# Block-diagonal attention matmuls, split input loads and DMA transposes in a fused linear-attention and MLP kernel

## The chip, the cores and the metric

The kernel runs on one core of a Trainium2 chip. The metric is the device time of the whole program in microseconds (us), the slowest core's, which here is the only core. The times quoted are medians of several executions. TensorE is called PE here, its weight loads PEld, VectorE DVE, ScalarE ACT, GpSimd POOL and SyncE SP. Every run also lists the mean granted TensorE clock, where 1.0 is full speed. A run that is over 1.5% above the fastest of its kernel counts as slow and is left out of the ratios; the others are the fast runs.

## The reference, cut to what matters

```python
# q, k, v: (8, 8, 576, 64) = (batch B, head H, token S, D), float32
q_s = softmax(q, axis=-1)                              # over D
k_s = softmax(k, axis=2)                               # over tokens
kv  = np.einsum('bhsd,bhse->bhde', k_s, v)             # 64 x 64 a head
o   = np.einsum('bhsd,bhde->bhse', q_s, kv)
x   = o.transpose(0, 2, 1, 3).reshape(4608, 512)       # heads side by side
h   = x @ w_in                                         # 512 x 2048
g   = np.where(h > 0, h, np.exp(np.minimum(h, 0)) - 1) # ELU
out = g @ w_out                                        # 2048 x 512
```

Nearly all arithmetic is in the two MLP products: 9 blocks of 512 tokens, 64 matmuls of 128x512 for the hidden layer and 64 for the output in each, 1152 in all.

## The kernel before

A *unit* is four heads of one batch, so there are 16 units, n = 0 to 15. The MLP runs in groups of eight matmuls: `hg(j, g)` is a hidden group of block j, `out_mm` an output group. The attention of later batches is put between those groups as *pieces*: transposes of q (`tp`), the product k^T v (`kv`), and two output pieces (`ao`). A small list scheduler inside the program fixes the order of instructions on each engine ahead of time, from assumed durations and an assumed DMA rate.

The load of q, k or v of a unit is one transfer of 590 KB (576 KB in the profile's units) that fills all 128 partitions. Partition half f (64 partitions) holds the heads f and 2+f of the four, one in each slot h:

```python
def load(self, n, t, key, eng="gp"):
    b, u = n // 2, n % 2
    i = n % 2
    src = self.src[t][b, 4 * u:4 * u + 4, :, :].rearrange(
        "(h f) (p c) d -> (f p) h (c d)", f=2, c=CH)      # head = 2h + f
    dst = self.RAW[i][t][:, :, :, :].rearrange("p h c d -> p h (c d)")
    # [cut] self.S.add(eng, ..., e.dma_start(dst, src), ...)
```

The order of two heads, f and 2+f, in one column block means that their outputs belong to different 128-row chunks of x. So the output piece uses four matmuls in row tiles of 64 partitions, which put heads 2h and 2h+1 together:

```python
def ao(self, n, x, ps, key, evac="act"):
    # [cut]
    for f in range(2):
        for h in range(2):
            hs = slice(h * 64, h * 64 + 64)
            e.matmul(P[:, h * 512:h * 512 + n_], M[hs, f, :],
                     T[hs, c0:c1, f * 64:f * 64 + 64], start=(f == 0), stop=(f == 1))
```

`kv` is called once a unit, 36 small matmuls each. `tp` makes nine PE transposes and one ACT eviction a unit. Loads, and the weights W1 and W2 behind them, stand in one POOL queue in the order of use; only q of unit 0 goes through SP.

The softmax here doesn't subtract the row's maximum and nothing guards it: scores larger than these inputs give would overflow.

## Time and profile before

| | before |
|---|---|
| time, median of 3 | 329.84 us (329.71 to 330.46) |
| span of the profiled execution | 328.2 us, clock 1.0 |
| first MLP matmul | 18.62 us |
| PE busy | 95% |
| PE waits after the first MLP matmul | 5.7 us (sum of the waits view from 18.7 us on) |

The waits of PE, longest in total first (total us, times, longest). The first two belong to the head of the program, with 0.2 us more of it not shown; the waits after the first MLP matmul sum to 5.7:

```profile
PE PS L354 <- ACT QR L320: 5.5, 1, 5.5
PE PS L385 <- ACT VB L331: 1.9, 1, 1.9
PE PS L444 <- DVE GT L459: 1.4, 2, 1.1
PE PS L475 <- DVE GT L465: 1.3, 1, 1.3
```

A unit of attention in steady state, from the timeline of PE (start, length, line, operation, tile, count): two output pieces, transposes and kv stand between MLP groups, and the groups beside the pieces last 2.09 to 2.12 us, where undisturbed ones (from 203.02 us on) last 1.98 and start 1.81 us apart.

```profile
183.34 0.50 PE L417 MATMUL PS<-qsT,MBLK 64*128 64x256 f32 x4
183.78 2.12 PE L444 MATMUL PS<-XT,W 128*128 128x512 f32 x8
185.74 0.68 PE L367 MATMUL PS<-ID,QS 128*128 128x128 f16 x9
186.22 2.09 PE L475 MATMUL PS<-W,GT 128*128 128x512 f32 x8
188.25 0.48 PE L385 MATMUL PS<-VB,KR 64*64 64x65 bf16 x36
188.66 2.12 PE L444 MATMUL PS<-XT,W 128*128 128x512 f32 x8
```

### The profile page before, as it was taken

Reading aid. Unit: us, or ns where it says so; the run is one execution under the profiler, and the core shown is the slowest. Engines: PE = TensorE matmul, PEld = TensorE weight load, DVE = VectorE, ACT = ScalarE, POOL = GpSimd, SP = SyncE. Lnnn points to the kernel's source line nnn. Section 1 sums busy time; section 2 is a strip of 40 time slices with the busy share of each in tenths; the row PEclk is TensorE's granted clock in tenths of the full one; section 3 lists DMA queues with packets and bytes.
Section 4 is the critical chain, followed back from the end, with each engine's and each line's share of the span. In section 5 each row is a group of like instructions: output and inputs, shape, how many; then the busy total and the mean of one; then the engine's idle time right before and its main releaser. Section 6 shows DMA issues by size and latency. Waiting matters only on the chain.

```text
span 328.2 us, 4867 instructions
## 1 busy us (share of the span) xinstructions
PE 310.5 (95%) x2090; PEld 241.3 (74%) x2090; DVE 191.2 (58%) x236; ACT 166.5 (51%) x190; POOL 70.7 (22%) x86
## 2 busy tenths in 40 slices
PE   3799999978999999999999999999999999999895
PEld 3677767655777776787778777877888888888683
DVE  4548844698877587667666546455455545554400
ACT  3835646996667467546744563444333343334211
POOL 8732443895403421304020020000000000000000
PEclk9999999999999999999999999999999999999999
DMA  7999999656636827623542130210121111112122
GB/s 235 396 386 389 390 358 323 191 178 211 206 121 217 247 42 241 213 70 104 176 149 61 34 105 7 56 35 13 39 49 32 32 34 32 32 34 59 37 64 64
DMA packets 17045, 46.45 MB, mean 142 GB/s; under 512 B 2048, under 2 KB 2048, under 8 KB 17024
## 3 DMA queue, kind: packets, MB, share of 16 engines
q0 software_dynamic: 10992, 36.11, 34.5%
q1 hardware_dynamic: 6032, 10.03, 12.2%
q8 instruction: 16, 0.26, 0.3%
q14 instruction: 5, 0.04, 0.0%
HBM read 36.70 MB, written 9.44 MB: 141 GB/s over the span
## 4 chain that ended last, share of the span: by engine, by line
PE 83%; DVE 7%; DMA 4%; ACT 3%; issue 1%; POOL 1%; SPq 0%; POOLq 0%
PE PS L475 39%; PE PS L444 36%; PE PS L417 4%; DMA VR<-in_v_dram 2%; DVE GT L459 2%; PE PS L367 2%; PE PS L385 2%; DMA out_dram<-OSB 1%; DVE QS L341 1%; ACT ESB L452 1%; DVE ZQ L333 1%; DVE GT L465 1%; POOL ESB L457 1%; ACT OSB L488 1%; PE PS L354 0%
## 5 line engine op out<-in xcount | busy, mean ns | idle before, releaser
L444 PE MATMUL PS<-XT,W 128*128 128x512 f32 x576 | 144.5, 395 | 2.8 <-DVE GT L459 1.4
L475 PE MATMUL PS<-W,GT 128*128 128x512 f32 x576 | 145.4, 396 | 1.3 <-DVE GT L465 1.3
L444 PEld LDWEIGHTS PS<-XT,W 128*128 128x128 f32 x576 | 106.0, 188 | 27.0 <-DVE GT L459 2.0
L475 PEld LDWEIGHTS PS<-W,GT 128*128 128x128 f32 x576 | 105.8, 188 | 25.6 <-issue 1.8
L452 ACT ACTIVATE ESB<-PS 128x1024 f32<-128x1024 f32 x72 | 73.8, 1026 | 89.8 <-PE PS L444 88.6
L463 DVE TENSOR_SCALAR ESB<-ESB 128x1024 f32<-128x1024 f32 x61 | 45.1, 740 | 70.1 <-ACT ESB L452 70.1
L465 DVE TENSOR_TENSOR GT<-ESB,PS 128x1024 fp32r<-128x1024 f32 x61 | 74.5, 1221 | 2.1
L488 ACT ACTIVATE OSB<-PS 128x512 f32<-128x512 f32 x36 | 21.5, 597 | 38.1 <-PE PS L475 36.1
L333 DVE TENSOR_REDUCE ZQ<-QR 128x18 f32<-128x1152 f32 x16 | 21.6, 1350 | 19.0 <-ACT QR L320 19.0
L320 ACT ACTIVATE QR<-QR 128x1152 f32<-128x1152 f32 x16 | 18.7, 1166 | 14.1 <-DMA QR<-in_q_dram 13.9
L328 POOL CAST VB<-VR 128x1152 bf16<-128x1152 f32 x15 | 18.4, 1230 | 31.7 <-PE PS L385 29.4
L293 POOL DMA_DIRECT2D QR<-in_q_dram x15 | 11.1, 738 | 64.8 <-DVE QS L341 57.3
L341 DVE TENSOR_TENSOR QS<-QR,RZQ 128x1152 f16<-128x1152 f32 x15 | 21.8, 1453 | 5.4 <-PE PS L367 5.2
L427 ACT ACTIVATE XT<-PS 128x640 fp32r<-128x640 f32 (+3 forms) x31 | 20.1, 650 | 7.1 <-PE PS L417 7.1
L370 ACT ACTIVATE qsT<-PS 128x1152 fp32r<-128x1152 f16 x15 | 17.0, 1130 | 6.3 <-PE PS L367 6.2
L324 ACT ACTIVATE KR<-KR 128x1152 bf16<-128x1152 f32 x16 | 18.6, 1161 | 1.8 <-DMA KR<-in_k_dram 1.7
L459 DVE SCALAR_TENSOR_TENSOR GT<-ESB,PS 128x1024 fp32r<-128x1024 f32 x11 | 13.4, 1217 | 6.0 <-POOL ESB L457 5.9
L417 PEld LDWEIGHTS PS<-qsT,MBLK 64*128 64x128 f32 x120 | 8.9, 185 | 10.2 <-issue 4.6
L417 PE MATMUL PS<-qsT,MBLK 64*128 64x320 f32 (+3 forms) x120 | 16.0, 345 | 0.0
L457 POOL TENSOR_SCALAR ESB<-ESB 128x1024 f32<-128x1024 f32 x11 | 12.3, 1119 | 15.3 <-ACT ESB L452 15.2
L293 POOL DMA_DIRECT2D KR<-in_k_dram x16 | 12.0, 748 | 7.3 <-PE PS L385 7.3
L354 PE MATMUL PS<-ID 128*128 128x128 f16 x90 | 7.3, 249 | 5.5 <-ACT QR L320 5.5
(30 smaller groups left out, 81.6 us busy)
## 6 DMA issues: line engine op xcount, KB each, us to landing
KR<-in_k_dram POOLq DMA_DIRECT2D x16, 576.0 KB, 5.2
VR<-in_v_dram POOLq DMA_DIRECT2D x16, 576.0 KB, 6.9
out_dram<-OSB SPq DMA_DIRECT2D x72, 128.0 KB, 2.4
QR<-in_q_dram POOLq DMA_DIRECT2D x15, 576.0 KB, 5.0
W<-in_moe_w_in_dram POOLq DMA_DIRECT2D x4, 1024.0 KB, 15.6
W<-in_moe_w_out_dram POOLq DMA_DIRECT2D x4, 1024.0 KB, 23.0
QR<-in_q_dram SPq DMA_DIRECT2D x1, 576.0 KB, 3.5
```

Source lines behind the costliest of these rows:

```text
L293: S.add(eng, ISSUE[eng], lambda e: e.dma_start(dst, src), key, W=[f"{t}R{i}"], dma=f"{t}{i}{eng}", nbytes=128 * 4608, follow=self.gpq if c ...
L333: S.add("dve", t_dve(1152), lambda e: e.tensor_reduce(self.ZQ[i][:, :, :].rearrange("p h c -> p (h c)"), raw["q"][:, :, :, :].rearrange("p ...
L341: S.add("dve", t_dve(1152), lambda e: e.tensor_tensor(qso, raw["q"][:, :, :, :], rz, ALU.mult), key - 3, R=rr("q") + [f"RZQ{i}"], W=[f"QS{ ...
L417: last = e.matmul(P[:, h * 512:h * 512 + n_], M[hs, f, :], T[hs, c0:c1, f * 64:f * 64 + 64], start=(f == 0), stop=(f == 1))
L427: S.add("act", t_act(2 * n_, True), lambda e: e.activation(dst, src, AF.Copy), key, W=W, X=banks)
L444: last = e.matmul(P[:, t * 512:(t + 1) * 512], self.W1[:, kc, tt * 128:(tt + 1) * 128], self.XT[:, kc, rc:rc + BLK], start=(kc == 0), stop ...
L452: S.add("act", t_act(1024, True), lambda e: e.activation(esb[:, :], P[:, :], AF.Exp), key, W=[f"E{i}"], X=banks)
L459: S.add("dve", t_dve(1024) + 60, lambda e: e.scalar_tensor_tensor(gt, esb[:, :], -1.0, P[:, :], ALU.add, ALU.max), key, R=[f"E{i}"], W=gw, ...
L463: S.add("dve", t_dve(1024, 2), lambda e: e.tensor_scalar(esb[:, :], esb[:, :], 1.0, -1.0, ALU.min, ALU.add), key, X=[f"E{i}"])
L465: S.add("dve", t_dve(1024) + 60, lambda e: e.tensor_tensor(gt, esb[:, :], P[:, :], ALU.max), key, R=[f"E{i}"], W=gw, X=banks)
L475: last = e.matmul(dst, GT[:, jj, ts * 128:(ts + 1) * 128], self.W2[:, jj, :], start=(jj == 0), stop=(jj == 15))
L488: S.add("act", t_act(512, True), lambda e: e.activation(osb[:, :], src, AF.Copy), key, W=[f"O{i}0", f"O{i}1"], X=[f"b{bk}"])
```

## The change

The intent is to take attention work off PE, the busiest engine. Two *adjacent* heads are put in one column block (head = 2f+h), so that one 128x128 block-diagonal matrix M replaces the tiled matmuls, two untiled matmuls for four tiled ones. `kv` runs once a batch (72 matmuls at once) from batch 2 on. The transposes of q from batch 2 on move to the DMA engines (issued from SP), with a POOL cast after them. The pieces stand at fixed steps of the MLP, and the scheduler's durations are new. The core of the diff:

```diff
-    def load(self, n, t, key, eng="gp"):
-        src = self.src[t][b, 4 * u:4 * u + 4, :, :].rearrange(
-            "(h f) (p c) d -> (f p) h (c d)", f=2, c=CH)
-        dst = self.RAW[i][t][:, :, :, :].rearrange("p h c d -> p h (c d)")
+    def load_half(self, n, t, f, eng, key, after=(), follow=None):
+        h0 = 4 * u + 2 * f
+        src = self.src[t][b, h0:h0 + 2, :, :].rearrange("h (p c) d -> p h (c d)", c=CH)
+        dst = self.RAW[i][t][f * 64:f * 64 + 64, :, :, :].rearrange("p h c d -> p h (c d)")
 ...
     def ao(self, n, x, ps, key, evac="act"):
-            for f in range(2):
-                for h in range(2):
-                    hs = slice(h * 64, h * 64 + 64)
-                    last = e.matmul(P[:, h * 512:h * 512 + n_], M[hs, f, :],
-                                    T[hs, c0:c1, f * 64:f * 64 + 64], start=(f == 0), stop=(f == 1))
+        for f in range(2):
+            def mm(e, f=f):
+                return e.matmul(P[:, f * 512:f * 512 + n_], M[:, f, :],
+                                T[:, c0:c1, f * 64:f * 64 + 64], start=True, stop=True)
 ...
+        if dmat:                                   # batches 2 to 7
+            t16 = self.raw_flat(i, "q").bitcast(F16)[:, 0:1152].rearrange("p (c t) -> p c t", c=CH)
+            S.add("sp", ISSUE["sp"], lambda e: e.dma_start_transpose(
+                t16, self.QS[al][:, :, :].rearrange("p c x -> p (c x)")), key, ...)
 ...
+        for m, (n, t) in enumerate(order):         # the head: units 0 and 1
+            sp = first[n, t] = self.load_half(n, t, 0, "sp", -70 + m, follow=sp)
+            ac = self.load_half(n, t, 1, "act", -70 + m, follow=ac)
+        self.load_w1(0, -60, after=[first[0, "v"]])
 ...
+            self.load_half(n, t, 1, "gp", ...)     # units 2 to 15
+            self.load_half(n, t, 0, "sp", ...)
```

With head = 2f+h the 128 partitions of a load no longer step evenly through memory, so the one transfer becomes two, each to 64 partitions. The bytes are the same.

## The prediction

> **What bounds it now.** TensorE. The page's first part has PE busy 95% of 328.2 us, DVE 58%, ACT 51%, at full clock. The timeline shows a head of 18.62 us before the first MLP matmul, 305.5 us of middle, and a tail of 4.0 us. Undisturbed groups of eight MLP matmuls start 1.81 us apart (203 to 216 us), so the 1152 need 261 us: a floor. Of the other 44 us of the middle about 6 are PE waits (waits view) and 37 attention on PE: at 183.3 to 193.2 us one unit (four heads) costs 9.89 - 4 x 1.81 = 2.63 us, 14 times. Transposes are 0.48 of it, kv 0.41, two output pieces 0.92; the other 0.8 is MLP groups stretched from 1.81 to about 2.04 us beside pieces, which I read as 0.09 on entering a tiled piece and 0.14 on leaving. [...]
>
> **What the change does.**
> - Output pieces: 2 untiled matmuls for 4 tiled ones[...]: 0.3 to 0.45 us against 0.46 plus 0.2.
> - kv once a batch: 0.82 + 0.23 us against 2 x (0.41 + 0.23).
> - Transposes of batches 2 to 7 leave PE (0.48 + 0.13 us a unit) and ACT (1.13 us). In their place: an SP-issued DMA transpose and a POOL cast of about 1.2 us. [...] The order leaves about 10.
> - So a batch costs PE 2.3 to 2.9 us, not 5.26: six save 14 to 18. Units 2 and 3 save 1.2.
> - DVE work is spread. The chain runs through DVE from 59 to 73 us and PE loses about 2.6 there; perhaps 2 come back.
> - New wait: after block 1, the second half output group follows the last hidden group by 2.2 us, while exp 1.03, POOL min 1.04 and DVE 1.22 need over 3.3: 1 to 1.5 us, once. Later boundaries leave 3.6 against 3.2: up to 0.5 each.
> - Head: v of unit 1 now reaches its matmul at 15.5 us, after a 1.16 us POOL cast. Loads on SP and ACT and a split cast should start the MLP at about 16: 2.5 saved.
> - Tail: two groups fill the 1.29 us wait before the last output; the last stores issue from two engines: 1.8 saved.
>
> **On the critical path.** Nearly all. Head 16 + MLP 261 + attention 20 + waits and small losses 5.5 + tail 3.5 = 306 us of span, plus 1.6 by which time exceeds span: 307.5 us, 7% less; range 302 to 313. Faster by over 2% 0.96, within 0.03, slower 0.01.
>
> **In the profile, if right.** First MLP matmul at 15.5 to 17 us. Groups beside output pieces at 1.81 us, stretched only around kv. Output matmuls start 0.15 to 0.23 us apart. [...] PE never waits behind the cast. A wait of 1 to 1.5 us after block 1, about 5 in all. The last wait of 1.29 gone.
>
> **What would make it wrong.** Slow DMA transposes; SP blocked behind them, and then stores, output buffers and PE; DVE slowed by POOL's added casts (a QS multiply takes 1.36 to 2.0 us); waits at every block boundary; ACT-issued loads delaying the head.

The 0.09 and 0.14 us are the estimate from the trace before, where groups beside tiled pieces last 2.09 to 2.12 us and undisturbed ones 1.98. "The order leaves about 10" means 10 us for a transpose and its cast. The sum: it adds up to 306 us of span, and with the 1.6 to 307.5 us (rounded).

## More of the kernel before

The page's first two parts. The first line gives busy time, share of the span and number of instructions; the others cut the span in 40 slices of 8.2 us, with busy tenths, granted clock in tenths, DMA engines' busy tenths, and the GB/s that moved:

```profile
PE 310.5 (95%) x2090; PEld 241.3 (74%) x2090; DVE 191.2 (58%) x236; ACT 166.5 (51%) x190; POOL 70.7 (22%) x86
...
PE   3799999978999999999999999999999999999895
...
PEclk9999999999999999999999999999999999999999
DMA  7999999656636827623542130210121111112122
GB/s 235 396 386 389 390 358 323 191 178 211 206 121 217 247 42 241 213 70 104 176 149 61 34 105 7 56 35 13 39 49 32 32 34 32 32 34 59 37 64 64
```

PE is the limit nearly everywhere. But read the last line too: from 8 to 49 us the DMA engines are full, at 358 to 396 GB/s, and PE only just gets its data. After some 60 us there is plenty of room.

The page's list of DMA issues, with KB each and the median us from issue to landing:

```profile
KR<-in_k_dram POOLq DMA_DIRECT2D x16, 576.0 KB, 5.2
VR<-in_v_dram POOLq DMA_DIRECT2D x16, 576.0 KB, 6.9
...
QR<-in_q_dram POOLq DMA_DIRECT2D x15, 576.0 KB, 5.0
...
W<-in_moe_w_out_dram POOLq DMA_DIRECT2D x4, 1024.0 KB, 23.0
```

## The result, and the profile after

The changed kernel is correct and takes 344.54 us (343.46 to 347.64, 4 runs), against 330.15 us (329.71 to 332.08, 4 runs) for the kernel before on the same chip. The ratio of the two is 1.044, with a 95% interval of 1.038 to 1.050: it is slower by 4.4%, where 6.8% faster was predicted. All ratios here are the mean time of one kernel's fast runs over the mean of the other's fast runs of the same rounds, so they are not quite the ratio of the medians. The granted clock was 0.964 or 0.965 in the runs of the changed kernel, and 1.0 in the profiled run before.

The same parts of the page:

```profile
PE 301.1 (88%) x1898; PEld 242.7 (71%) x1898; DVE 194.9 (57%) x240; ACT 152.0 (44%) x178; POOL 76.7 (22%) x93
...
PE   1689467678887988999999999999999999899995
...
PEclk9879959988999999999999999999999999999999
DMA  7999999987698589459656944841212111111133
GB/s 180 303 368 269 247 272 224 250 213 203 137 231 150 106 206 214 123 129 255 151 109 169 238 110 126 204 101 42 57 44 47 34 31 31 31 33 31 31 77 78
```

PE does less work, and in the first third it is idle more often and its granted clock is under 0.9 in five of the 13 slices, at the lowest 0.50 (42.7 to 51.3 us). The DMA engines are as busy as before there (9 tenths), but in four of the five slices from the second to the sixth they move 247 to 303 GB/s, where the kernel before moved 358 to 396. They are busy longer, for the same inputs. The list of issues: half the size, and hardly an earlier landing (q from POOL, not shown, takes 5.2 us):

```profile
QR<-in_q_dram SPq DMA_DIRECT2D x16, 288.0 KB, 4.8
KR<-in_k_dram SPq DMA_DIRECT2D x16, 288.0 KB, 6.5
VR<-in_v_dram SPq DMA_DIRECT2D x16, 288.0 KB, 8.5
W<-in_moe_w_out_dram POOLq DMA_DIRECT2D x4, 1024.0 KB, 29.7
...
KR<-in_k_dram POOLq DMA_DIRECT2D x14, 288.0 KB, 5.6
VR<-in_v_dram POOLq DMA_DIRECT2D x14, 288.0 KB, 6.8
```

The waits of PE. The second and the fifth line belong to the head. From the first MLP matmul on, at 23.22 us, they sum to 26.3 us (with the 0.6 us just before that matmul), against 5.7 before:

```profile
PE PS L516 <- DVE GT L499: 9.0, 2, 7.3
PE PS L467 <- ACT QR L323: 7.1, 1, 7.1
PE PS L483 <- DVE GT L506: 4.0, 5, 1.3
PE PS L483 <- ACT XT L459: 3.7, 1, 3.7
PE PS L399 <- POOL VB L363: 3.2, 1, 3.2
PE PS L516 <- DMA W<-in_moe_w_out_dram: 3.1, 1, 3.1
```

The longest wait, 7.3 us, is put down to DVE, but DVE is not its cause. The timelines of ACT and of PE (in brackets, the idle time before and what ended it) show the chain behind it:

```profile
41.08 1.16 ACT L323 ACTIVATE QR<-QR 128x1152 f32<-128x1152 f32 x1 [7.42 <-DMA QR<-in_q_dram]
42.14 1.92 ACT L491 ACTIVATE ESB<-PS 128x1024 f32<-128x1024 f32 x2
```

```profile
45.58 5.49 PE L516 MATMUL PS<-W,GT 128*128 128x512 f32 x12 [7.33 <-DVE GT L499]
```

In the program's order for ACT, the exponential of q of unit 2 stands ahead of two exponentials of MLP block 0, and ACT waits 7.4 us for its data; so the MLP exponentials, DVE after them, and PE after that, all wait for a load of q. The 12 matmuls after the wait then take 5.49 us, where 12 at full speed take 2.72 (12 times the 1.81/8 of an undisturbed group). The granted clock was 0.50 in that stretch (windows view, 45.5 to 51.1 us), and 0.56 in the 4.5 us before it, in which PE was idle; it had been 1.00 from 37 to 41 us. What lowers it, the runs do not show.

The chain of waits that ends last, in the stretch from 25 to 70 us, is made of loads of v and of W1 (start, length, what):

```profile
18.00 10.98 DMA W<-in_moe_w_in_dram
...
30.29 15.62 DMA VR<-in_v_dram
...
47.47 21.12 DMA VR<-in_v_dram
```

Later, PE does its work as fast as was predicted, or faster. A block of 16 MLP groups and one batch of attention takes 31.15 us (149.67 to 180.82), of which 16 x 1.814 = 29.02 is MLP, so this batch costs PE 2.13 us, against 2 x 2.63 = 5.26 before. The groups beside its output pieces last 1.98 to 2.01 us, like undisturbed ones; the one after kv lasts 2.11:

```profile
149.67 0.78 PE L399 MATMUL PS<-VB,KR 64*64 64x65 bf16 x72
150.38 2.11 PE L516 MATMUL PS<-W,GT 128*128 128x512 f32 x8
...
159.90 1.98 PE L483 MATMUL PS<-XT,W 128*128 128x512 f32 x8
161.72 0.41 PE L440 MATMUL PS<-qsT,MBLK 128*128 128x256 f32 x2
161.96 2.01 PE L516 MATMUL PS<-W,GT 128*128 128x512 f32 x8
```

So the picture is: the gain that was sought is there, 3.13 us a batch, or 18.8 us in all if all six batches are like this one, and then about 33 us were lost elsewhere, most of it before 110 us.

### The profile page after: what moved, and what is told of

Same layout as the page of the kernel before. It is cut to its first block, busy times and chain, and to the rows that moved or that the text cites. A ratio compares the mean times of both kernels' runs of the same rounds, so it can differ in the third digit from the quotient of the medians.

```text
span 341.7 us, 4607 instructions
## 1 busy us (share of the span) xinstructions
PE 301.1 (88%) x1898; PEld 242.7 (71%) x1898; DVE 194.9 (57%) x240; ACT 152.0 (44%) x178; POOL 76.7 (22%) x93
## 4 chain that ended last, share of the span: by engine, by line
PE 62%; DMA 22%; DVE 6%; POOL 3%; ACT 2%; issue 2%; SPq 2%; ACTq 0%; POOLq 0%
PE PS L516 31%; PE PS L483 29%; DMA VR<-in_v_dram 14%; DMA W<-in_moe_w_in_dram 3%; DMA QR<-QS 2%; DVE GT L506 2%; DMA out_dram<-OSB 2%; PE PS L440 2%; ACT ESB L491 2%; DMA QR<-in_q_dram 1%; SPq L284 1%; DVE ESB L503 1%; POOL VB L363 1%; DVE QS L333 1%; POOL qsT L347 1%
## 5 line engine op out<-in xcount | busy, mean ns | idle before, releaser
L516 PEld LDWEIGHTS PS<-W,GT 128*128 128x128 f32 x576 | 108.6, 192 | 35.3 <-DVE GT L499 9.9
L506 DVE TENSOR_TENSOR GT<-ESB,PS 128x1024 fp32r<-128x1024 f32 x63 | 76.9, 1221 | 2.2
L347 POOL CAST qsT<-QR 128x1152 fp32r<-128x1152 f16 x12 | 15.4, 1285 | 88.5 <-PE PS L440 73.1
L357 ACT ACTIVATE KR<-KR 128x1152 bf16<-128x1152 f32 x16 | 18.5, 1164 | 12.5 <-DMA KR<-in_k_dram 12.4
L363 POOL CAST VB<-VR 128x1152 bf16<-128x1152 f32 x15 | 17.5, 1191 | 12.8 <-DMA VR<-in_v_dram 12.8
L459 ACT ACTIVATE XT<-PS 128x640 fp32r<-128x640 f32 (+4 forms) x30 | 18.6, 620 | 1.4 <-PE PS L440 1.4
L440 PE MATMUL PS<-qsT,MBLK 128*128 128x320 f32 (+5 forms) x64 | 14.9, 321 | 4.2 <-ACT XT L459 2.5
L440 PEld LDWEIGHTS PS<-qsT,MBLK 128*128 128x128 f32 x64 | 12.1, 198 | 8.6 <-ACT XT L459 3.6
L284 POOL DMA_DIRECT2D KR<-in_k_dram x14 | 9.3, 666 | 39.2 <-PE PS L399 39.2
L496 POOL TENSOR_SCALAR ESB<-ESB 128x1024 f32<-128x1024 f32 x9 | 9.9, 1097 | 20.9 <-ACT ESB L491 20.9
L499 DVE SCALAR_TENSOR_TENSOR GT<-ESB,PS 128x1024 fp32r<-128x1024 f32 x9 | 11.0, 1220 | 6.1 <-POOL ESB L496 6.0
L412 DVE RECIPROCAL RZK<-PS 128x2 f32<-128x2 f32 x16 | 2.7, 168 | 19.9 <-PE PS L399 19.7
```

The costliest lines, as they stand in the source:

```text
L347: self.S.add("gp", 1250, lambda e: e.tensor_copy(dst, src), key, R=[f"qR{i}0", f"qR{i}1"], W=["qsT0"], low=True, tag=f"cvt{n}")
L363: S.add("gp", 1250, lambda e: e.tensor_copy(VB[:, :, :, 0:D], raw[:, :, :, :]), key, R=rv, W=[f"VB{i}0", f"VB{i}1"], low=True, tag=f"cv{n}")
L440: return e.matmul(P[:, f * 512:f * 512 + n_], M[:, f, :], T[:, c0:c1, f * 64:f * 64 + 64], start=True, stop=True)
L506: S.add("dve", t_dve(1024), lambda e: e.tensor_tensor(gt, esb[:, :], P[:, :], ALU.max), key, R=[f"E{i}"], W=gw, X=self.banks(ps), tag=f"el ...
L516: last = e.matmul(dst, GT[:, jj, ts * 128:(ts + 1) * 128], self.W2[:, jj, :], start=(jj == 0), stop=(jj == 15))
```

## The experiments

The theories:

- **T1**: the loads are slow because each transfer fills 64 of the 128 partitions.
- **T2**: they are slow because of the queues that issue them (SP and ACT in place of POOL).
- **T3**: they are not slow; they only come in a bad order, or the engines' order is wrong. A later form, **Theory B** against it, says that the data come too late at any order.
- **T4**: the DMA transposes disturb the loads.

### e1: the loads by themselves

A measuring kernel, with a wrong output, repeats the loads of units 0 and 1 (3.54 MB) in eight forms, one after the other, with waits between, then the DMA transposes.

```diff
+ full loads:  POOL | SP | SP and ACT
+ half loads:  SP + ACT | SP + POOL | both POOL | both SP | lower half only, SP
+ DMA transposes of q, SP
```

> A measuring kernel, wrong output on purpose: ten phases of loads alone, each begun when the one before has landed. T1 (a load that fills only 64 of 128 partitions is slow): the full loads of phases 1 to 3 run at about 390 GB/s on any queue, the lower halves alone (phase 8) at about 200 to 235, and halves from two queues (4, 5) in between. T2 (the SP and ACT queues are slower than POOL's): phases 2, 3, 4 and 8 at about 235, phases 1 and 6 (both from POOL) at about 390. T3 (rates are equal, only order and gates differ): every phase at about 390 GB/s. Phases 9 and 10: transposes land in 3 to 4 us alone, and slow the loads beside them by no more than their bytes if they are harmless.

The windows view, in the order above (stretch and length; busy time of DVE and POOL, with nothing of note; clock; DMA engines' busy share; GB/s):

```profile
...
18.00:24.00 6.00, 0.00 (x0) 0.00 (x0) 1.00 1.03 380
30.00:36.00 6.00, 0.00 (x0) 0.00 (x0) 1.00 1.05 401
42.00:50.00 8.00, 0.00 (x0) 0.00 (x0) 1.00 1.05 281
...
91.00:101.00 10.00, 0.00 (x0) 0.00 (x0) 1.00 1.04 234
107.00:112.00 5.00, 0.00 (x0) 0.00 (x0) 1.00 1.04 208
116.00:121.00 5.00, 0.00 (x0) 0.00 (x0) 1.00 0.97 220
```

Three forms are left out of the fence: whole loads from POOL, whose first issue still lies in the stretch that was read (350 GB/s), halves on SP and POOL (286), and both halves on POOL (235). The whole transfers move 380 to 401 GB/s from SP or SP and ACT, so the queues are not at fault and T2 falls. Halves move 281 to 286 when two queues carry one half each, 234 to 235 from one queue, and 208 when only one half is loaded. In all of them the DMA engines are busy all the time (1.03 to 1.05). So the engines are not idle; each byte takes longer. T3, that the loads are not slow, falls as a whole explanation too. The last line of the fence is the transposes alone; phase 10, transposes beside loads, is read under e6.

One queue with both halves gave 234 against 208 for one half alone, 13% more, and two queues gave 281, 35% more, though far from 401. Why half of the partitions, or half of the size, is slower, no run here shows.

### e2: whole loads in the changed kernel

Each pair of half loads becomes the wide load of the kernel before. Heads are then paired wrongly and the output is wrong; the work is the same. The edit also takes the later loads off SP, and with them the wait for W1 that the SP halves had, so e2 alone does not part the form of the loads from their order; e1 and e3 are needed beside it.

```diff
-    self.load_half(n, t, 1, "gp", key); self.load_half(n, t, 0, "sp", key)
+    self.load_full(n, t, "gp", key)     # "(h f) (p c) d -> (f p) h (c d)", 128 partitions
```

> The changed kernel with each q, k and v load as one 128-partition load (SP and ACT in turn in the head, POOL later); heads are paired as before, so the output is wrong on purpose. T1: most of the loss comes back, head at 17 to 18 us, PE waits between 35 and 80 us under 6 us, time 308 to 318 us. T2: the head stays at about 22 us and only the later stalls go: about 325. T3 (it is the order of pieces and gates): 338 us or more.

The fast runs were 319.88 and 320.58 us, a ratio of 0.970 [0.966, 0.973] to the kernel before. Two more runs, 326.93 and 327.93, count as slow. So by its fast runs the change with whole loads is 3% faster than the kernel before, and about 24 us faster than with half loads (17 us by the slow ones). That lies between the theories' numbers: T1 expected 308 to 318 us and a head of 17 to 18 us (20.14 measured), T2 about 325 us and a head of 22. The DMA line of the page is again like that of before, up to 390 GB/s, and the clock is full:

```profile
PEclk9999999999999999999999999999999999999999
DMA  7999998954965644783595437313111112011132
GB/s 278 292 351 390 388 390 319 283 137 152 257 154 151 246 120 129 245 194 97 120 289 174 112 82 218 109 33 72 33 33 36 33 44 51 7 33 33 46 86 69
```

PE's waits after the head are 12.5 us in place of 26.3 (in both with the 0.6 us just before the first MLP matmul).

### e3: half loads in the kernel before

The other direction: the kernel before, with only its loads split by partition half. It is correct, since the order of heads is kept.

```diff
-    e.dma_start(dst, src)                       # 128 partitions, POOL
+    for f, eng in ((0, "sp"), (1, "gp")):       # 64 partitions each
+        e.dma_start(RAW[f * 64:f * 64 + 64], src[f])
```

> The kernel before with each load cut into a lower half from SP and an upper half from POOL, all else the same. T1: the head and the first 80 us become slow as in the changed kernel, 338 us or more. T2: half of the bytes slow, about 335. T3: within 1% of before.

It took 359.72 us (357.76 to 360.23), a ratio of 1.087 [1.083, 1.092]: the split, with half of each load moved to SP, costs the kernel before 29 us. PE then waits for W1 (4.4 us) and W2 (4.8 us), which stand behind the slow loads. e1, e2 and e3 together show the split loads as the main cause: they are slow by themselves, taking the split away gives back 24 us, and putting it into the other kernel costs 29. That it is the 64 partitions of T1, and not the smaller size of each transfer, e2 and e3 do not tell apart (see e13).

### e4 and e5: which loads

e4 has whole loads for units 0 and 1 only, e5 for units 2 to 15 only. Both outputs are wrong, as in e2.

```diff
 e4: - load_half(n, t, 0, "sp"); load_half(n, t, 1, "act")     # head only
     + load_full(n, t, "sp" or "act")
 e5: - load_half(n, t, 1, "gp"); load_half(n, t, 0, "sp")      # all but the head
     + load_full(n, t, "gp")
```

> The changed kernel with full loads for units 0 and 1 only (wrong output on purpose for these); the later loads stay halves from SP and POOL. By the half-load theory the head falls from 23.2 to about 20.1 us and the stalls between 38 and 80 us stay: 340 to 342 us, so the head is the small part of the loss.

> The changed kernel with halves for units 0 and 1 only, full loads from POOL later (wrong output on purpose). Head about 23 us as in the changed kernel, the stalls after it mostly gone: 322 to 326 us. If instead head and later losses only shift into each other, this and the run with a full head both stay near 340.

e4: 343.77 us, ratio 1.041 [1.035, 1.047], within a us of the changed kernel. e5: 325.83 us, ratio 0.985 [0.979, 0.991]. e5 is as expected, though "unclear" as a verdict at 2%. In e4 the first MLP matmul came at 21.8 us, not at 20.1, and what was gained was lost in the next wait, a single one of 12.9 us, before which ACT waits 9.3 us for q of unit 2. So the head alone brings nothing. The loads after the head bring 19 us, and the head 5 us more on top of them (e2).

### e6: PE transposes in place of DMA transposes

e2, with the transposes of batches 2 to 7 back on PE and their eviction on ACT (output wrong, as in e2). The pieces move to other steps to make room for them.

```diff
-    self.q_part(n0, first_step, True);  self.cvt(n0, first_step)
+    self.q_part(n0, first_step, False); self.tp(n0, AT, key)
```

> All loads full as in e2, and the transposes of batches 2 to 7 put back on PE with an ACT eviction. If DMA transposes are as good as free there, this is slower than e2's fast runs (320) by the PE time of 12 transposes, 12 x 0.48 to 0.61 = 6 to 7 us: about 326. If the transposes' small packets or the POOL cast cost time in e2, it is slower by less, or faster.

328.01 us (327.14 to 329.05), about 8 us above e2's fast runs. So with whole loads the DMA transposes are worth their place. And in the changed kernel the first of them leaves at 78.93 us, after the late head and after 16.6 of the 26.3 us of PE's waits, so T4 cannot be the cause of that part of the loss.

But transposes beside loads are not harmless. Alone a transpose lands in 2.9 us (e1, phase 9). In phase 10 two transposes and four whole loads, 2.96 MB in all, took 20 us (121.6 to 141.6), where the rates measured alone, 220 and 380 GB/s, give an estimate of 9; one transpose landed after 5.3 us and one after 16.9. "No more than their bytes" was missed, and no run tells why. In the changed kernel transposes land in 2.9 to 8.1 us; how much of its 9.1 us of waits after 79 us is theirs was not tested.

### e7: whole loads only at the start

A first correct try at a better kernel: units 0 to 3 with whole loads and the tiled output pieces of the kernel before, half loads and the block-diagonal form from batch 2 on; head on SP; pieces of unit 3 earlier.

```diff
+NOLD = 4                              # units below: load_full, 4 tiled ao matmuls
-            6: lambda: (self.ao(2, 0, AT, key), loads(4, "kv", key)),
+            5: lambda: (self.ao(2, 0, AT, key), loads(4, "kv", key)),
```

> A correct version: units 0 to 3 with full loads and the tiled output matmuls of before, the head's loads all on the SP queue in order, halves with block-diagonal matmuls from batch 2 on, pieces of unit 3 one step earlier, the first output groups of block 1 reordered to give the last hidden group 3.6 us, block 8 starting with one hidden group. If half loads cost only while DMA is the limit (first 60 us), this is faster than e2: head 17 us, 309 to 315 us. If halves hurt in the steady part too, 318 or more.

327.45 us, ratio 0.994 [0.986, 1.002]: the same as the kernel before. The first MLP matmul came at 17.5 us. But waits of 3.4, 2.5 and 2.3 us stayed, the first of them with ACT waiting 3.3 us for q of unit 2 while MLP exponentials stand behind it. That q is a whole load, so this wait is not one for halves, and the time, outside the 309 to 315 us expected, does not tell what halves cost later.

### e8: the right rates in the ordering model

The changed kernel with no other work and no other loads, but with the scheduler told that a half load takes 1.65 times its bytes' time, and a transpose 1.7 times.

```diff
-    dma=f"{t}{i}{f}{eng}", nbytes=64 * 4608,
+    dma=f"{t}{i}{f}{eng}", nbytes=int(64 * 4608 * 1.65),
-    dma="tp", nbytes=128 * 2304
+    dma="tp", nbytes=int(128 * 2304 * 1.7)
```

> The changed kernel with its loads as they are, but the order of instructions worked out with the load and transpose rates that were measured: the bytes that the ordering model counts for a half load are scaled by 1.65 and for a transpose by 1.7. Same work, correct output. Theory A (late loads stall PE mostly because in-order ACT and DVE queues were ordered for landings at 370 GB/s, so that an exp of q that waits for its load holds up the MLP's exps): the 7 us wait of PE at 38 us goes and the time falls by 5 to 12 us, to 333 to 340. Theory B (the data are simply too late whatever the order): within 1.5% of the changed kernel, 340 to 347.

345.43 us (341.08 to 346.60), ratio 1.040 [1.031, 1.048]: no gain, where Theory A expected 333 to 340 us. The 7.3 us wait is gone, but others have taken its place, as the waits view shows (the first line is 3.3 us of the head and 1.7 after it):

```profile
PE PS L399 <- POOL VB L363: 5.0, 2, 3.3
PE PS L516 <- DMA W<-in_moe_w_out_dram: 5.0, 1, 5.0
PE PS L440 <- DVE MBLK L417: 4.2, 1, 4.2
```

This speaks for Theory B: while the bytes come too late, this order moved the waits. It does not prove it, for one order is not every order: the waits after the first MLP matmul fell from 26.3 to 21.1 us, but that matmul came at 24.83 us in place of 23.22, and from 20 to 30 us the clock was 0.50 in place of 0.95. The long wait of 7.3 us *looks* like an ordering mistake, and mending it brought nothing.

### e9 and e10: whole loads for three batches or for two, with the right rates

As e7, with the order made for measured rates, W1 in four pieces and issued earlier (after k of unit 0), and the cast of v of unit 0 on ACT; e9 keeps whole loads and tiled pieces for units 0 to 5, e10 for units 0 to 3.

```diff
+NOLD = 6       # e9; e10: 4
-DMA_RATE = 370.0
+DMA_RATE = 300.0
+# M is zeroed again where the form changes
```

> A correct version: batches 0 to 2 with full loads and tiled output matmuls, head loads on SP in order, W1 issued once k of unit 0 has landed, halves with block-diagonal matmuls and DMA transposes from batch 3 on, order worked out with 300 GB/s and the scaled bytes. Theory A: no wait of ACT for q between the MLP's exps of block 0; head 16.5 to 17.5 us, PE waits after it under 6 us, 308 to 315 us. If waits over 2 us stay in blocks 0 to 2, 318 or more.

> As e9 but only batches 0 and 1 with full loads; batch 2's halves are loaded between 40 and 75 us, beside W2. If halves hurt only where DMA is the limit, batch 2's still lie partly in that stretch: 1 to 5 us slower than e9. If the choice of batch 2 makes no difference, within 1 us, or faster by its cheaper output matmuls (about 2 us).

e9: 322.17 us (321.33 to 322.95), ratio 0.973 [0.969, 0.978]. e10: 323.61 us, ratio 0.978 [0.974, 0.982], "unclear" at the bound of 2%. Both are correct, and faster than both kernels. Neither reached the 308 to 315 us of Theory A; e10 is 1.4 us slower than e9, as was expected if halves hurt where DMA is the limit. The head of e9 was late (22.2 us) and block 0 ran throttled (clock 0.61 from 20 to 30 us).

### e11 and e12: the same with the head of the kernel before

```diff
-    first[n, t] = self.load_full(n, t, "sp", -70 + m, follow=sp)
+    first[n, t] = self.load_full(n, t, "gp" if m else "sp", -70 + m, follow=self.gpq ...)
-    self.load_w1(0, -60, after=[first[0, "k"]])
+    self.load_w1(0, -60)
```

> As e9 (full loads and tiled attention matmuls for batches 0 to 2, the block-diagonal form from batch 3), but the head's loads go in one queue in the order of the kernel before (q of unit 0 alone on SP; q1, k0, v0, k1, v1, then W1, on POOL). If the head of e9 (first MLP matmul at 22.2 us and a throttled block 0) is what kept it at 322 us: first MLP matmul at 18.5 to 19.5 us, block 0 at full clock, 313 to 318 us. If the head is not the cause, it stays at 320 or above although the first MLP matmul comes earlier, and the waits between 30 and 100 us grow instead.

> The same, with full loads and tiled attention for batches 0 and 1 only, so block-diagonal form from batch 2. If split loads from batch 2 on still land in time, it gains the 2.5 us or so of one batch's PE work over e11: 311 to 317 us. If the split loads of batch 2 are still inside the stretch in which the DMA engines are the limit, it is as slow as e11 or slower by 1 to 3 us, as e10 was against e9 (323.6 against 322.2).

e11: four runs of 321.85 (fast), 328.57, 330.26 and 333.85 us (slow). e12: 326.08 us (325.65 to 326.69), ratio 0.989 [0.986, 0.992]. Both expectations failed. In both, block 0 ran at full clock (1.00 from 20 to 30 us, where e9 had 0.61), so the head was mended (18.4 and 18.3 us), and the total was no better. In the profiled run of e11, a slow one, a single wait of 6.2 us for a transposed q came in its place, and the clock fell to 0.83 between 60 and 80 us. The gain at the head was given back later, as in e4. The four runs of this one binary spread over 12 us.

### e13, e14 and e15: another split

A single transfer cannot take this order of heads in one even step over 128 partitions; but each *slot* h can, if the partition half is made an extra outer step. So the load is split by slot and not by partition half: again two transfers of the same size from the same queues, now over all 128 partitions. The output is correct.

```diff
-    src = self.src[t][b, h0:h0 + 2].rearrange("h (p c) d -> p h (c d)", c=CH)
-    dst = self.RAW[i][t][f * 64:f * 64 + 64]
+    src = self.src[t][b, 4 * u:4 * u + 4].rearrange("(g h) (p c) d -> h g p (c d)", g=2, c=CH)[f]
+    dst = self.RAW[i][t][:, f]         # f now counts the slot
 e14: head in the order of the kernel before;  e15: also pieces one step earlier, rate 300
```

> The changed kernel with one edit: each q, k or v load is still two transfers of 295 KB from the same two queues, but split by the head slot (h) and not by the partition half (f), so that each fills all 128 partitions; correct output. If the 64-partition form is what makes the loads slow: DMA at 350 to 390 GB/s between 20 and 45 us, and a time near the wide loads of e2, 318 to 325 us. If the number or the size of transfers is at fault: 340 us or more, as the changed kernel, with under 320 GB/s.

> e13 with the head's loads in the order of the kernel before: slot 0 on SP and slot 1 on POOL (slot 1 of the first q on ACT), W1 behind them without a gate in four pieces of 1 MB, the casts of v of unit 0 on ACT and of unit 1 on POOL as before. If the order of the head's loads is what makes e2's head 20.1 us: first MLP matmul at 18 to 19 us, and 1 to 3 us less than e13. If not, within 1 us of e13.

> e14 with the pieces of units 2 and 3 one step earlier, the first output groups of block 1 in the order 0, 2, 1, 3, the last block alternating from its first step, and the order made for a DMA rate of 300 in place of 370. If the remaining PE waits of e2 (3.6, 2.8, 2.4 and 1.9 us) come of where the pieces stand: PE waits after the head under 8 us in all, 312 to 317 us. If they come of late data at any order: within 2 us of e14.

They took 570.91, 549.52 and 546.04 us. No theory had expected this. The windows view of e13 while only these loads are under way (same columns as in e1, with all engines):

```profile
10.00:40.00 30.00, 4.93 (x53) 4.76 (x53) 2.98 (x3) 2.65 (x3) 0.00 (x0) 0.87 0.13 51
```

The DMA engines' share (next to last) is 0.13, as much as the busy time of 2 of 16 engines, and 51 GB/s move; from 10 to 48 us the SP queue and the ACT queue each took 6.5% of the 16 engines' span, as much as one engine. Why this split keeps them so little busy, no run shows; but the half loads of e1 had a share of 1.03 to 1.05, so the fault here is another one. The experiment therefore does not tell partitions from the size of transfers, as it was meant to. One number speaks against size: the 36 stores of 256 KB at the end of e1, smaller than a half load but over all 128 partitions, move 382 GB/s from SP alone. They are stores and not loads, so the question stays open. e13 separates two different faults: a busy share of 0.13 with 51 GB/s (e13), and a busy share of 1.03 to 1.05 with 208 to 286 GB/s in place of 380 to 401 (e1).

### e16 and e17: wide loads and the right heads

e16 keeps the wide load, so that heads f and 2+f share a matrix, and puts each result in its right chunk when it leaves PSUM: four evictions of 64 partitions a piece, two on ACT and two on DVE, in place of one on ACT. The rest is the changed kernel. The output is correct. e17 adds the head of the kernel before, earlier pieces and a rate of 330.

```diff
-    dst = self.XT[:, 2 * u:2 * u + 2, x0:x0 + n_]                 # one eviction, 128 partitions
+    for f, eng in ((0, "act"), (1, "dve")):
+        for h in range(2):
+            dst = self.XT[f * 64:f * 64 + 64, 2 * u + h, x0:x0 + n_]
+            s = src[h * 64:h * 64 + 64, f, :]
```

> The changed kernel with the wide loads of the kernel before (128 partitions, one transfer, DMA engines all in use) and a correct result: the attention output is evicted in four pieces of 64 partitions, two on ACT and two on DVE, each to its right place. If the split loads were the miss: 318 to 326 us, as e2 (320.6), with DMA at 380 to 395 GB/s between 20 and 45 us. If something else of the changed kernel was, 335 us or more. The four evictions cost ACT and DVE about 0.3 us more a piece, which should stay off PE's path.

> e16 with the head's loads in the order of the kernel before (one POOL queue, q of unit 0 on SP), pieces of units 2 and 3 one step earlier, block 1's first output groups in the order 0, 2, 1, 3, the last block alternating from its first step, and the order made for a DMA rate of 330. If e2's rest over the prediction was head and order: first MLP matmul at 18 to 19 us, PE waits after it under 8 us, 312 to 317 us. If not: within 2 us of e16.

e16: 329.91 us (328.36 to 332.06), ratio 0.999 [0.993, 1.005], between the 318 to 326 us expected if the split loads were the miss and the 335 expected if not. e17: 319.14 us in its one fast run, 324.23, 328.12 and 330.17 in slow ones (312 to 317 us were expected). So a correct kernel with wide loads is 14.6 us faster than the changed kernel (344.54 less 329.91), not the 24 us of e2. The difference from e2 is the evictions: they add 29.2 us of DVE (64 of 456 ns), 0.9 us a piece where 0.3 was expected, and PE waits 4.7 us once for DVE's write of M. Just before that write, at 76.27 us, one TENSOR_SCALAR of DVE took 4.36 us (median 0.69) while POOL ran casts; why is not shown. That the evictions are the whole difference was not tested apart.

## Why the prediction was wrong, point by point

**The step that failed.** The prediction says of the head: "Loads on SP and ACT and a split cast should start the MLP at about 16: 2.5 saved." And its sum has "waits and small losses 5.5". Both take the bandwidth of the loads as unchanged, since the bytes are. It did not cost the split. Measured, halves move 281 to 286 GB/s from two queues where whole loads move 380 to 401 (e1). From 8 to 49 us the DMA engines were already full before the change, so the slower loads showed as a late head, 23.22 us in place of 16, and as waits of PE, 26.3 us in place of 5.5.

| term of the sum | predicted | changed kernel | e2, whole loads |
|---|---|---|---|
| first MLP matmul, us | 16 | 23.22 | 20.14 |
| PE waits after it (with the 0.6 just before), us | 5.5 | 26.3 | 12.5 |
| tail, us | 3.5 | 3.6 | not read |
| time, us | 307.5 | 344.54 | 320.2 (mean of two fast runs) |

Of the 37.0 us that the changed kernel is over the prediction, the head is 7.2 and the waits are 20.8, together 28.0. The 12 matmuls at 45.58 us took 2.8 us more than at full clock, and 32 at 78.29 us took 9.18 in place of 7.25, 1.9 more; the granted clock was 0.50 and 0.82 there, after waits of 7.3 and 3.65 us. The remaining 4.3 us are not divided further.

**Where the loss was right before the eye.** "What would make it wrong" names "ACT-issued loads delaying the head" and slow DMA transposes, but not the split. The queues were not the fault (e1), and with whole loads the transposes were worth 8 us (e6).

**PE's work: right, a little low.** "So a batch costs PE 2.3 to 2.9 us, not 5.26": measured 2.13 in one batch. The groups beside its untiled pieces last 1.98 to 2.01 us, where undisturbed ones last 1.98; the one after kv lasts 2.11. A piece of two matmuls holds PE for 0.24 to 0.29 us there before the next group starts, so its matmuls start about 0.12 to 0.15 us apart, at or below the low end of what was predicted.

**The wait after block 1: right in kind, a little low.** Predicted 1 to 1.5 us, once; measured 1.65 at 105.06 us. Later boundaries: 0.24 to 0.94 against "up to 0.5 each".

**The last wait: wrong in place.** "The last wait of 1.29 gone": a wait of 1.29 us stands at 296.02 us, at the start of the last block.

**PE never waits behind the cast: nearly right.** It waited 0.2 us. The transposes landed in 2.9 to 8.1 us (median 3.6).

**What would still be wrong with fast loads.** e2 is 12.7 us over the prediction. The head is 4.1 of it, the waits after the head 7.0 (12.5 less 5.5). In e2's head the loads of both units' q leave from two queues at once and land together, and the exponential of q starts at 5.77 us, against 4.31 before. So the head would not have come at 16 us in any case that was run; the best, 17.5, was e7's. Nor is e2's 20.14 firm: e6, with the same loads in the head, started the MLP at 21.98 us.

**What stays open.** Whether half loads are slow for their 64 partitions or for their size is not settled (e13), nor what the DMA transposes cost beside loads (phase 10 of e1). Whether a correct kernel with all loads whole can reach e2's 320 us is not shown: e17's one fast run did (319.14), three others did not. Which term makes the runs of e2, e11 and e17 spread over 8 to 12 us was not found; their mean granted clock goes from 0.969 to 1.0. The best version with a verdict is e9, 322.17 us, 2.7% faster than the kernel before.

## What to carry to other kernels

Before a change of layout is costed by its instructions, look at what it does to the shape of the transfers: the same bytes over 64 of 128 partitions took 1.3 to 1.7 times as long here (380 to 401 GB/s against 234 to 286), with DMA engines that look fully busy, and the split by head slot took the rate down to 51 GB/s, at a busy share of 0.13 (e13). Read GB/s beside the busy share, and find the stretches in which DMA is already full: there, a slower transfer made a longer kernel, and the one other order that was tried did not hide it (e8). When a mended wait brings nothing (e4, e8, e11), suspect that the limit is behind it, and let the next experiment change the supply and not the order.
